# A windowed attention with block summaries and a four-expert attention layer: from a scheduled program to a recorded order of steps on fixed engines

## The chip, the cores and the metric

One core of a Trainium2 chip runs the whole program. The metric is the device time of one execution in microseconds. It is compared between two kernels that compute the same thing from the same inputs.

## The reference

Two layers follow each other. Batch 4, 8 heads, 768 positions, head size 64; the second layer has 4 experts of head size 64 over a model width of 512.

```
# layer 1, per head: local window plus block summaries
k_sum = k.reshape(B, H, 24, 32, D).max(axis=3)      # 24 blocks of 32 keys
v_sum = v.reshape(B, H, 24, 32, D).mean(axis=3)
scores = [where(|i - j| < 16, q k^T / 8, -1e9),  q k_sum^T / 8 + log(32)]
x = softmax(scores) @ [v, v_sum]                    # heads side by side: x is 768 x 512
# layer 2, per expert e: causal attention; a token uses its 2 best experts
logits = x @ w_gate;  w = softmax over the 2 largest logits
ye = softmax(causal(q_e k_e^T / 8)) @ v_e @ wo[e]   # q_e, k_e, v_e = x @ wq[e], wk[e], wv[e]
out = sum over the chosen e of w_e * ye
```

The choice of the two experts is exact in effect, so the kernels carry x as a half-precision high part and a low part (`xT_hi`, `xT_lo`), and the gate's logits use both.

## The kernel before

The kernel is written as Python loops over batches (L336). Each batch has a stage 1 (L114, layer 1) and a stage 2 (L215, layer 2). A scheduler places the instructions by data and by priority in program order; the engine of each instruction is the one that the code names, and the buffers come from pools with a fixed number per name (L52 to L56). PSUM has two tags of tiles: `one` (one bank, four buffers) and `two` (two banks, two buffers).

**Stage 1** works on head pairs, four per batch. For four heads at a time, v is loaded with 32 rows of a block per partition and reduced by a tree of five additions on GpSimd (L118 to L126): the block sums of v. Per pair, q and k are loaded and cast to half precision by GpSimd's DMA queue, one DMA per head (L133), in pieces of 256 bytes; windows of v (96 rows for each block of 64 queries) come by SP's queue (L142, L145), and the block sums are copied below them (L148). TensorE transposes q and k (L153, L158), VectorE copies them out of PSUM and takes the block maxima of k (`ksum`, L162). Scores are built in a two-bank tile per head: a mask is written by a matmul with the identity (L171), 12 local matmuls add the 96 keys of the windows (L178), and two matmuls with `ksum` as the stationary add the 24 summaries (L184). ScalarE takes the exponential of 120 rows (L188). The value matmul (L196) uses the exponentials as the stationary in fp32; VectorE normalises (L200, L201); TensorE transposes x (L206); ScalarE writes the high part (L209) and VectorE the low part (L210).

**Stage 2** projects values and gate logits (L224, L227), computes the gates in a chain of small VectorE steps with one exponential (L247 to L259), and handles two experts (`cc`) at a time: projections of q and k (L268), scores for three groups of key tiles and one expert after the other (L288), exponentials (L293), a causal select on the diagonal blocks by GpSimd (L298), the value matmuls (L307), normalisation times gate (L310 to L313), and transposes (L317). The output projection (L325) is copied by ScalarE or VectorE and stored by SP's queue (L332).

Stage 2's weights are loaded once, after stage 1 of batch 0 in program order, by GpSimd's queue with a cast (L83 to L99).

Of the kernel before, what the change touches and what calls it, by code (L numbers as in the profile page):

```python
# [8 lines left out]
FP32 = mybir.dt.float32  # L9
HALF = mybir.dt.float16  # L10
AL = mybir.AluOpType
# [19 lines left out]

GROUPS = [[(0, 0), (4, 768)], [(1, 0), (3, 640)], [(2, 0), (5, 512)]]
GBASE = [0, 1024, 2048]
GLEN = [1024, 1024, 640]
OFF2 = {tj: GBASE[g] + col for g, grp in enumerate(GROUPS) for tj, col in grp}

def win_start(t):
    return min(max(64 * t - 16, 0), S - WIN)
# [3 lines left out]
def kernel(  # L43
# [6 lines left out]
    nc = tc.nc  # L50

    consts = ctx.enter_context(tc.tile_pool(name="consts", bufs=1))  # L52
    xpool = ctx.enter_context(tc.tile_pool(name="xpool", bufs=2))
# [5 lines left out]
    ident16 = consts.tile((128, 128), HALF, name="ident16")  # L59
    make_identity(nc, ident16)  # L60
    ident32 = consts.tile((128, 128), FP32, name="ident32")
    make_identity(nc, ident32)

    maskb = consts.tile((128, NQ, 64), HALF, name="maskb")
    nc.gpsimd.memset(maskb, 0.0)
    for t0, t1 in ((0, 1), (1, NQ - 1), (NQ - 1, NQ)):
        shift = 64 * t0 - win_start(t0)
        m = maskb[0:WIN, t0:t1, :]
        n = t1 - t0

        nc.gpsimd.affine_select(m, m, [[0, n], [-1, 64]], AL.is_ge, NEG,
                                base=15 - shift, channel_multiplier=1)
        nc.gpsimd.affine_select(m, m, [[0, n], [1, 64]], AL.is_ge, NEG,
                                base=15 + shift, channel_multiplier=-1)

    wqk = consts.tile((128, NCH, 2, 2, 128), HALF, name="wqk")
    wvg = consts.tile((128, NCH, 264), HALF, name="wvg")
    wo_cat = [consts.tile((128, 512), HALF, name=f"wo_cat{cc}") for cc in range(2)]
    wg_f32 = consts.tile((128, NCH, 4), FP32, name="wg_f32")
    wg_hi32 = consts.tile((128, NCH, 4), FP32, name="wg_hi32")  # L80
    wg_lo32 = consts.tile((128, NCH, 4), FP32, name="wg_lo32")

    def load_stage2_weights():  # L83
        nc.sync.dma_start(out=wg_f32,
                          in_=moe_w_gate.rearrange("(c p) g -> p c g", p=128))
        for e in range(E):
            cc, ep = divmod(e, 2)
            for j, wsrc in enumerate((moe_wq, moe_wk)):
                nc.gpsimd.dma_start(out=wqk[:, :, cc, j, 64 * ep:64 * ep + 64],
                                    in_=wsrc[e].rearrange("(c p) d -> p c d", p=128))  # L90
            nc.gpsimd.dma_start(out=wvg[:, :, 64 * e:64 * e + 64],
                                in_=moe_wv[e].rearrange("(c p) d -> p c d", p=128))
        for cc in range(2):
            nc.gpsimd.dma_start(out=wo_cat[cc],
                                in_=moe_wo[2 * cc:2 * cc + 2].rearrange("e d n -> (e d) n"))
        nc.vector.tensor_copy(wvg[:, :, 256:260], wg_f32)
        nc.vector.tensor_copy(wg_hi32, wvg[:, :, 256:260])
        nc.vector.tensor_tensor(wg_lo32, wg_f32, wg_hi32, AL.subtract)
        nc.vector.tensor_scalar(wvg[:, :, 260:264], wg_lo32, LO_SCALE, None, AL.mult)  # L99
# [271 lines left out]
```

## Time and profile before

| | |
|---|---|
| runs, median (lowest to highest) | 301.04 us (299.4 to 301.61), 3 runs |
| profiled execution, span | 298.8 us |
| mean granted TensorE clock | 0.859 |
| TensorE / VectorE / ScalarE / GpSimd busy | 218.1 / 123.0 / 96.0 / 127.1 us |
| moved by DMA | 32.10 MB in 109,001 packets |

The span is the time from the first to the last instruction of the profiled execution; the page gives no other time for it. Busy time is the time in which an engine executes an instruction, and shares are of the span. The granted clock is a share of TensorE's full clock of 2.4 GHz: 1.00 is 2.4 GHz, 0.50 is 1.2 GHz, and numbers between them are a mean over the stretch. Matmuls are pipelined, so the start of one to the start of the next says more than the duration of one. "issue" is time in which an engine waited for nothing that the profile shows.

### The profile page before, as it was taken

Reading aid. Unit: us, or ns where it says so; the run is one execution under the profiler, and the core shown is the slowest. Engines: PE = TensorE matmul, PEld = TensorE weight load, DVE = VectorE, ACT = ScalarE, POOL = GpSimd, SP = SyncE. Lnnn points to the kernel's source line nnn. Section 1 sums busy time; section 2 is a strip of 40 time slices with the busy share of each in tenths; the row PEclk is TensorE's granted clock in tenths of the full one; section 3 lists DMA queues with packets and bytes.
Section 4 is the critical chain, followed back from the end, with each engine's and each line's share of the span. In section 5 each row is a group of like instructions: output and inputs, shape, how many; then the busy total and the mean of one; then the engine's idle time right before and its main releaser. Section 6 shows DMA issues by size and latency. Waiting matters only on the chain.

```text
span 298.8 us, 5906 instructions
## 1 busy us (share of the span) xinstructions
PE 218.1 (73%) x2448; PEld 140.8 (47%) x2448; DVE 123.0 (41%) x280; ACT 96.0 (32%) x117; POOL 127.1 (43%) x191
## 2 busy tenths in 40 slices
PE   1004998492678798877978888697789799679683
PEld 0002766360245466653544666462555566545340
DVE  0002655348042456654407366361425555461231
ACT  1001233205325433316261333307242433225612
POOL 7998543599603444892134249903024000003110
PEclk9999999867587999998675999976867999895957
DMA  7899999993920999939205999993009300000005
GB/s 199 124 81 173 169 168 191 135 119 50 176 49 0 155 232 220 171 79 177 56 0 39 309 225 103 157 184 70 2 0 133 133 2 2 2 0 2 0 0 211
DMA packets 109001, 32.10 MB, mean 107 GB/s; under 512 B 104880, under 2 KB 105136, under 8 KB 108208
## 3 DMA queue, kind: packets, MB, share of 16 engines
q0 software_dynamic: 56800, 7.35, 38.5%
q1 hardware_dynamic: 52176, 24.39, 37.7%
q8 instruction: 19, 0.31, 0.4%
q14 instruction: 6, 0.05, 0.1%
HBM read 30.42 MB, written 6.29 MB: 123 GB/s over the span
## 4 chain that ended last, share of the span: by engine, by line
PE 46%; DVE 22%; ACT 12%; POOL 9%; DMA 5%; issue 4%; SPq 0%; ACTq 0%; POOLq 0%
PE sp L288 7%; PE pp L268 6%; POOL v_s L123 6%; PE av L196 6%; PE av L307 6%; DVE xT_lo L210 5%; ACT a L293 4%; PE op L325 4%; PE sc L178 4%; ACT aT L188 4%; DVE ksum L162 4%; DVE x L201 4%; PE vp L224 3%; PE sc L171 3%; DMA v_s<-in_v_dram 3%
## 5 line engine op out<-in xcount | busy, mean ns | idle before, releaser
L298 POOL TENSOR_SCALAR_AFFINE_SELECT a<-a 128x256 f16<-128x256 f16 x48 | 19.4, 406 | 102.5 <-ACT a L293 102.5
L293 ACT ACTIVATE a<-sp 128x1024 f16<-128x1024 f32 (+1 forms) x48 | 41.2, 921 | 13.4 <-PE sp L288 13.4
L188 ACT ACTIVATE aT<-sc 120x768 f32<-120x768 f32 x32 | 25.5, 810 | 54.3 <-PE sc L184 54.3
L133 POOL DMA_DIRECT2D q_nat<-in_q_dram x32 | 26.9, 850 | 36.8 <-PE qT_ps L153 31.6
L123 POOL TENSOR_TENSOR v_s<-v_s 96x1024 f32<-96x1024 f32 (+4 forms) x40 | 40.6, 1023 | 3.4 <-DMA v_s<-in_v_dram 1.8
L288 PE MATMUL sp<-qkT,qkT 64*128 64x512 f16 (+3 forms) x128 | 27.8, 364 | 19.0 <-ACT a L293 10.4
L196 PE MATMUL av<-v_blk,aT 120*64 120x65 f32 x768 | 29.8, 231 | 5.1 <-ACT aT L188 2.9
L196 PEld LDWEIGHTS av<-v_blk,aT 120*64 120x64 f32 x768 | 25.9, 143 | 12.4 <-ACT aT L188 7.0
L307 PEld LDWEIGHTS <-a 128*128 128x128 f16 x336 | 20.3, 129 | 21.1 <-POOL a L298 17.8
L307 PE MATMUL av<-v,a 128*128 128x65 f16 x336 | 25.5, 242 | 5.1 <-POOL a L298 5.0
L209 ACT CAST xT_hi<-xT_ps 128x768 f16<-128x768 f32 x16 | 12.8, 798 | 47.4 <-PE xT_ps L206 47.4
L310 DVE RECIPROCAL r<-av 128x6 f32<-128x6 f32 x16 | 3.0, 190 | 60.6 <-PE av L307 60.6
L133 POOL DMA_DIRECT2D k_nat<-in_k_dram x32 | 26.7, 854 | 1.5 <-DMA k_nat<-in_k_dram 1.5
L200 DVE RECIPROCAL rec<-av 128x6 f32<-128x6 f32 x32 | 6.3, 196 | 50.5 <-PE av L196 50.5
L268 PE MATMUL pp<-xT_hi,wqk 128*128 128x512 f16 (+1 forms) x128 | 27.0, 358 | 0.0
L178 PEld LDWEIGHTS <-kT 64*96 64x96 f16 x384 | 18.8, 126 | 10.4 <-issue 5.7
L171 PE MATMUL sc<-maskb,ident 128*128 128x512 f16 x64 | 16.1, 337 | 10.3 <-DVE xT_lo L210 5.0
L178 PE MATMUL sc<-qT,kT 64*96 64x64 f16 x384 | 22.3, 212 | 0.6 <-DVE kT L160 0.6
L224 PE MATMUL vp<-wvg,xT_hi 128*128 128x264 f16 x96 | 19.1, 342 | 4.8 <-DMA wvg<-in_moe_wv_dram 3.1
L288 PEld LDWEIGHTS <-qkT 64*128 64x128 f16 x128 | 8.8, 98 | 28.0 <-issue 12.0
L153 PE MATMUL qT_ps<-ident,q_nat 128*128 128x128 f16 x96 | 9.4, 244 | 15.7 <-DMA q_nat<-in_q_dram 15.7
L325 PE MATMUL op<-wo_cat,wT 128*128 128x512 f16 x48 | 19.1, 536 | 1.1 <-DVE wT L319 0.7
(62 smaller groups left out, 272.1 us busy)
## 6 DMA issues: line engine op xcount, KB each, us to landing
v_blk<-in_v_dram SPq DMA_DIRECT2D x32, 240.0 KB
v_s<-in_v_dram SPq DMA_DIRECT2D x8, 768.0 KB
out_dram<-o_sb SPq DMA_DIRECT2D x12, 512.0 KB
q_nat<-in_q_dram POOLq DMA_DIRECT2D x32, 96.0 KB, 5.3
k_nat<-in_k_dram POOLq DMA_DIRECT2D x32, 96.0 KB, 6.5
v_blk<-v_s SPq DMA_DIRECT2D x32, 72.0 KB
v_blk<-in_v_dram SPq DMA_DIRECT2D x32, 48.0 KB
wqk<-in_moe_wq_dram POOLq DMA_DIRECT2D x4, 64.0 KB, 13.3
```

Of the source, the lines that this page charges most:

```text
L123: nc.gpsimd.tensor_tensor(v_s[:, 0:half], v_s[:, 0:half], v_s[:, half:2 * half], AL.add)
L133: nc.gpsimd.dma_start(out=dst[:, :, 64 * hp:64 * hp + 64], in_=src[b, 2 * c + hp].rearrange("(t p) d -> p t d", p=128))
L171: nc.tensor.matmul(sc[:, lo:hi], ident16, maskb.rearrange("p t n -> p (t n)")[:, lo:hi], start=True, stop=False, skip_group_check=True)
L178: nc.tensor.matmul(sps[hp][0:WIN, 64 * t:64 * t + 64], kT[rows, w0:w0 + WIN], qT[rows, 64 * t:64 * t + 64], start=False, stop=False, skip_ ...
L188: nc.scalar.activation(aT[0:KR, :], sps[hp][0:KR, 0:S], AF.Exp, scale=SCALE)
L196: nc.tensor.matmul(av[o:o + 64, t // 2, :], aTs[hp][0:KR, 64 * t:64 * t + 64], v_blk[0:KR, hp, t, :], start=True, stop=True)
L224: nc.tensor.matmul(vp[:, i, 0:264], xT_hi[ch][:, cols], wvg[:, ch, :], start=(ch == 0), stop=False, skip_group_check=True)
L268: nc.tensor.matmul(pp[:, lo:hi], wqk[:, ch, cc, j, :], xT_hi[ch][:, lo:hi], start=(ch == 0), stop=(ch == NCH - 1))
L288: nc.tensor.matmul(sp[:, c0:c0 + w], kT[rows, 128 * tj:128 * tj + 128], qT[rows, n0:n0 + w], start=True, stop=True)
L293: nc.scalar.activation(a2s[ep][:, base:base + ln], sp[:, 0:ln], AF.Exp, scale=SCALE / (XS * XS))
L307: nc.tensor.matmul(av2[:, ti, :], a2s[ep][:, o:o + 128], v2[:, tj, e, :], start=(tj == 0), stop=(tj == ti))
L325: nc.tensor.matmul(op[:, i, :], wavT[cc][:, 2 * t2 + i, :], wo_cat[cc], start=(cc == 0), stop=(cc == 1))
```

## The change

The loops and the scheduler's order are replaced by a list of 734 steps, each with the buffers that it reads and writes (`Plan`), and a table with one entry per step: its number, its engine (V VectorE, A ScalarE, G GpSimd, S SP, P TensorE) and the slots of the buffers that it opens. The steps are issued in the order of the table, and the scheduler is told to keep that order. The table interleaves stage 1 of a batch with stage 2 of the batch before. Copies that were always on one engine are divided among VectorE and ScalarE, and the additions of the v tree among GpSimd and VectorE.

The steps themselves change too. q and k are loaded four heads at a time, with 6 (q) or 8 (k) neighbouring positions in one partition, so that a piece is 1,536 or 2,048 bytes; a pair then needs 12 transposes for q and 16 for k, each filling 64 output partitions, and the copies out of PSUM put q's columns back in order. k stays in its order, and a copy (`kw`) gathers for each block of 64 queries its window of 96 keys, beside which the 24 block maxima are placed: one stationary of 128 columns. The summary matmuls go. The masks are matmuls over 64 rows per head. One DMA per pair loads the v windows of both heads. In stage 2 the score units are of at most 512 columns for both experts, whose matmuls alternate. Weights are loaded in fp32 by SP and cast by engines. PSUM is one tile of eight banks.

```diff
+UNITS = [[(0, 0, 512)], [(0, 512, 256), (4, 512, 256)], [(1, 128, 512)],
+         [(1, 640, 128), (3, 384, 384)], [(2, 256, 512)], [(5, 640, 128)]]
+UORDER = [0, 2, 4, 3, 1, 5]
...
+TABLE = """
+19,S,0 4,G, 5,V, 20,V, 17,G,0 88,P,0.0 6,G, 21,V, 8,G, 22,V, 68,P,1.1 0,G,1 18,G,0 89,V, 91,A,0 73,P,0.0 3,G,1
...
+    def emit(self, table):
...
+        for i, eng, slots in table:
...
+            st.fn(eng)
...
+                    nc.gpsimd.dma_start(
+                        out=T[name + "n"][t.slot][:, n * i:n * i + n, :],
+                        in_=src[b, h0:h0 + n].rearrange("h (p s) d -> p h (s d)", s=s))
...
+        def tk(e):
+            src = T["kn"][kn[b, g].slot]
+            for s in range(8):
+                for hp in range(2):
+                    nc.tensor.transpose(pbank16(kp)[64 * hp:64 * hp + 64, 96 * s:96 * s + 96],
+                                        src[:, hh + hp, 64 * s:64 * s + 64], T["id16"][0:96, 0:96])
...
+            copy(e, w[:, 1:NQ - 1, 0:WIN].rearrange("c t (p s) -> c t p s", s=8), src(6, 10, 8, 12))
...
+            copy(e, T["kw"][kw.slot][:, :, WIN:KR],
+                 T["ks"][ks.slot].unsqueeze(1).to_broadcast((128, NQ, NSUM)))
...
+                        nc.tensor.matmul(s[:, hp, 64 * t0:64 * t1], T["mt"][r, var, :],
+                                         T["pi"][r, t0:t1, :],
+                                         start=(i == 0), stop=False, skip_group_check=True)
+                for t in range(6):
+                    for hp in range(2):
...
+                        nc.tensor.matmul(s[:, hp, 64 * t:64 * t + 64],
+                                         T["kw"][kw.slot][r, tt, :],
+                                         T["qT"][qT.slot][r, 64 * tt:64 * tt + 64],
+                                         start=False, stop=True, skip_group_check=True)
...
+                    for tj, n0, w in UNITS[u]:
+                        for ep in range(2):
+                            r = slice(64 * ep, 64 * ep + 64)
+                            nc.tensor.matmul(pbank(sp, 2)[:, ep, c0:c0 + w],
+                                             T["qk"][qk[1].slot][r, 128 * tj:128 * tj + 128],
+                                             T["qk"][qk[0].slot][r, n0:n0 + w],
+                                             start=True, stop=True)
...
-    s1 = ctx.enter_context(tc.tile_pool(name="s1", bufs=2))
-    s2 = ctx.enter_context(tc.tile_pool(name="s2", bufs=2))
-    ps = ctx.enter_context(tc.tile_pool(name="ps", bufs=2, space=bass.MemoryType.PSUM))
...
+    ctx.enter_context(tc.manual_schedule())
...
+    T["ps"] = ps.tile((128, 8, 512), FP32, name="ps")
...
+    R = make_plan(nc, T, q, k, v, moe_w_gate, moe_wq, moe_wk, moe_wv, moe_wo, out)
+    R.emit(decode(TABLE))
```

## Rows read from the trace of the kernel before

**Rows 1.** The page: busy us of each engine, share of the span, instructions.

```profile
PE 218.1 (73%) x2448; PEld 140.8 (47%) x2448; DVE 123.0 (41%) x280; ACT 96.0 (32%) x117; POOL 127.1 (43%) x191
```

**Rows 2.** Stretches: length, busy us and instructions by engine, clock, DMA share, GB/s.

```profile
165.80:194.40 28.60, 23.49 (x376) 17.23 (x375) 15.01 (x29) 9.57 (x12) 19.92 (x22) 1.00 1.25 191
194.40:230.70 36.30, 30.70 (x238) 17.73 (x239) 14.40 (x41) 14.16 (x17) 8.28 (x17) 0.72 0.55 74
293.80:298.80 5.00, 0.00 (x0) 0.00 (x0) 0.00 (x0) 0.98 (x1) 0.00 (x0) 0.78 0.66 257
...
110.00:117.17 7.17, 6.42 (x100) 4.65 (x100) 4.29 (x8) 2.42 (x4) 3.29 (x4) 1.00 1.73 202
194.70:197.70 3.00, 3.00 (x25) 2.17 (x26) 0.83 (x3) 0.00 (x0) 0.00 (x0) 0.51 1.78 181
197.70:198.80 1.10, 1.10 (x21) 0.97 (x20) 0.84 (x3) 0.00 (x0) 0.00 (x0) 1.00 1.49 199
208.95:210.70 1.75, 1.75 (x33) 1.75 (x32) 0.56 (x3) 0.00 (x0) 0.28 (x1) 0.50 0.03 9
```

**Rows 3.** Timeline of the start: start, us, engine, line, operation, idle before.

```profile
6.61 2.33 POOL L123 TENSOR_TENSOR v_s<-v_s 96x1024 f32<-96x1024 f32 x1 [1.29 <-DMA v_s<-in_v_dram]
...
21.94 0.80 PE L153 MATMUL qT_ps<-ident,q_nat 128*128 128x128 f16 x6 [15.67 <-DMA q_nat<-in_q_dram]
```

**Rows 4.** Timeline of TensorE over one head pair.

```profile
109.93 0.72 PE L178 MATMUL sc<-qT,kT 64*96 64x64 f16 x12
110.58 0.49 PE L184 MATMUL sc<-qT,ksum 64*24 64x512 f16 x2
111.00 1.95 PE L196 MATMUL av<-v_blk,aT 120*64 120x65 f32 x48
112.88 0.51 PE L153 MATMUL qT_ps<-ident,q_nat 128*128 128x128 f16 x6
113.23 0.50 PE L158 MATMUL kT_ps<-ident,k_nat 128*128 128x128 f16 x6
113.96 0.84 PE L206 MATMUL xT_ps<-ident,x 128*128 128x128 f32 x6 [0.23 <-DVE x L201]
114.64 0.49 PE L171 MATMUL sc<-maskb,ident 128*128 128x512 f16 x2
```

**Rows 5.** The chain that ended last, two pieces: start, us, what.

```profile
209.15 1.76 PE av L307 x32
...
263.76 1.33 PE pp L268 x8
```

**Rows 6.** Groups by line, VectorE and ScalarE: busy us, mean ns, idle before.

```profile
L293 ACT ACTIVATE a<-sp 128x1024 f16<-128x1024 f32 x32 | 30.8, 1026 | 11.9 <-PE sp L288 11.9
L188 ACT ACTIVATE aT<-sc 120x768 f32<-120x768 f32 x32 | 25.5, 810 | 54.3 <-PE sc L184 54.3
L201 DVE TENSOR_TENSOR x<-av,rec 128x384 f32<-128x384 f32 x32 | 17.8, 557 | 1.1
L210 DVE TENSOR_TENSOR xT_lo<-xT_ps,xT_hi 128x768 f16<-128x768 f32 x16 | 15.3, 956 | 7.5 <-ACT xT_hi L209 7.4
L162 DVE TENSOR_REDUCE ksum<-kT 128x24 f16<-128x768 f16 x16 | 15.2, 953 | 0.5
L155 DVE COPY qT<-qT_ps 128x768 f16<-128x768 f16 x16 | 8.8, 550 | 22.9 <-PE qT_ps L153 22.8
```

**Rows 7.** Groups by line, GpSimd.

```profile
L298 POOL TENSOR_SCALAR_AFFINE_SELECT a<-a 128x256 f16<-128x256 f16 x48 | 19.4, 406 | 102.5 <-ACT a L293 102.5
L123 POOL TENSOR_TENSOR v_s<-v_s 96x1024 f32<-96x1024 f32 x8 | 18.9, 2362 | 1.8 <-DMA v_s<-in_v_dram 1.8
```

**Rows 8.** DMA: queues with packets, MB, share; issues with KB, us to landing.

```profile
q0 software_dynamic: 56800, 7.35, 38.5%
q1 hardware_dynamic: 52176, 24.39, 37.7%
...
k_nat<-in_k_dram POOLq DMA_DIRECT2D x32, 96.0 KB, 6.5
```

More of the change, by code (lines that the diff above doesn't have):

```diff
@@ L6 @@
 from concourse._compat import with_exitstack
-from concourse.masks import make_identity
 FP32 = mybir.dt.float32
@@ new lines, with __init__, buf, step @@
+class Plan:
+    def __init__(self):
+        self.steps = []
+    def buf(self, cls, n=1):
+        return Buf(cls, n)
+    def step(self, name, opts, reads, writes, fn, mode=0, dma=0.0, keep=()):
+        for x in set(reads) | set(writes) | set(keep):
+            x.left += 1
+        self.steps.append(Step(name, opts, reads, writes, keep, fn, mode, dma))
+    def emit(self, table):
+        held = set()
+        for i, eng, slots in table:
+            st = self.steps[i]
+            used = [x for x in dict.fromkeys(list(st.reads) + list(st.writes) + list(st.keep))
+                    if not x.cls.startswith(".")]
+            new = [x for x in used if x.slot is None]
+            assert len(slots) == len(new), st.name
+            for w, s in zip(new, slots):
+                w.slot = s
+                for k in range(w.n):
+                    assert (w.cls, s + k) not in held, (st.name, w.cls, s)
+                    held.add((w.cls, s + k))
+            st.fn(eng)
+            for x in set(st.reads) | set(st.writes) | set(st.keep):
+                x.left -= 1
+                if x.left == 0 and x.slot is not None:
+                    for k in range(x.n):
+                        held.remove((x.cls, x.slot + k))
@@ L42, with decode @@
+def decode(text):
+    out = []
+    for w in text.split():
+        i, e, s = w.split(",")
+        out.append((int(i), e, [int(x) for x in s.split(".") if x]))
+    return out
 @with_exitstack
@@ L336, with one, many @@
-    for b in range(B):
-        x = stage1(b)
-        if b == 0:
-            load_stage2_weights()
-        stage2(b, *x)
+    ctx.enter_context(tc.manual_schedule())
+    sb = ctx.enter_context(tc.tile_pool(name="sb", bufs=1))
+    ps = ctx.enter_context(tc.tile_pool(name="ps", bufs=1, space=bass.MemoryType.PSUM))
+    T = {}
+    def one(name, shape, dt):
+        T[name] = sb.tile(shape, dt, name=name)
+    def many(name, shape, dt):
+        T[name] = [sb.tile(shape, dt, name=f"{name}{i}") for i in range(SLOTS[name])]
@@ new lines @@
+    one("id16", (128, 128), HALF)
+    one("id32", (128, 128), FP32)
+    one("mt", (128, 3, 128), HALF)
+    one("pi", (128, 6, 64), HALF)
+    one("wqk", (128, NCH, 2, 2, 128), HALF)
+    one("wvg", (128, NCH, 264), HALF)
+    one("wo", (128, 2, 512), HALF)
+    one("wg32", (128, NCH, 4), FP32)
+    one("wgt", (128, NCH, 4), FP32)
+    many("qn", (128, 4, 384), HALF)
+    many("kn", (96, 4, 512), HALF)
+    many("kT", (128, S), HALF)
+    many("ks", (128, NSUM), HALF)
+    many("kw", (128, NQ, 128), HALF)
```

781 lines of the change are left out of this document (518 added, 263 removed).

## The prediction

> **What bounds the kernel now.** I read the page's engine shares first, because they say whether one engine is full. TensorE is busy 73% of the 298.8 us span, VectorE 41%, ScalarE 32%, GpSimd 43% [rows 1]. No engine is full, so the loss is in how the work is lined up, and the next view is the stretches [rows 2]. There each batch alternates: 28.6 us of stage 1 with TensorE 82% busy at granted clock 1.00, then 36 us of stage 2 with it 85% busy, but at clock 0.72. A busy TensorE at the lower of its two levels (1.2 instead of 2.4 GHz) is only half used, and the reader can see it on one kind of work: 25 matmuls of the value projections take 3.00 us at 0.51, and 21, mostly the same, 1.10 us at 1.00 [rows 2]. So stage 2 is long because ScalarE's exponentials and the copies make TensorE wait, and because the waiting lowers its clock. Last I read the start [rows 3]: both v loads are reduced on GpSimd ahead of its first q load, and the first transpose is at 21.94 us.
>
> **The change part by part.** I sum TensorE at clock 1.00, then add start, end and stalls; every instruction count is from the diff.
>
> *Stage 1, per head pair (16 pairs).* Now [rows 4]: 12 transposes at 0.35 us for six (112.88 to 113.23), 58 ns each; twice 0.42 masks, 0.65 for 12 local matmuls (109.93 to 110.58) and 0.42 summary (to 111.00; the masks have the same 768 columns), 2.98 together; 48 value passes in 1.95; output transposes 0.68. That is 6.3, beside 6.42 busy in 7.17 [rows 2].
> - Transposes become 28, each filling one half of the output partitions, 1,536 columns in each half. Below: the halves run side by side, 1,536 columns at 2.4 GHz, 0.64. Above: 28 x 58 ns, 1.62. The nearest row is the value matmul, which also alternates between output halves: 1.95 us / 48 = 40 ns, so I take 28 x 0.040 = 1.12. The Trainium skill's TensorEngine Tiling (Performance Considerations) says that column tiling switches off the fast weight load, and its page TensorE: Matmul & The Clock Gate (LDWEIGHTS) prices a load at columns/1.2 ns, an estimate of 53 ns here; by that this term would be 1.5 and the total some 6 us more, but the 40 ns of the value passes, 64 columns wide too, speak against it.
> - Scores: the four summary matmuls go (2 x 0.42), since a block's stationary now holds its 96 local keys and the 24 summaries. The 24 local ones stay, with 128 columns of weights instead of 96. Below, 64 columns at 2.4 GHz are 27 ns; above, 58; the row gives 54 (0.65/12). I take the middle, 40: 0.97. Masks: the same 1,536 columns, but each over half the rows: 0.32 (side by side) to 0.84 (today); I take 0.42. Together 1.4, bounds 0.96 and 2.2.
> - Values 1.95 and output transposes 0.70 stay.
>
> Sum 1.12 + 1.4 + 1.95 + 0.70 = 5.17, bounds 4.25 and 6.5; 16 pairs: 83 us (68 to 104), today about 101.
>
> *Stage 2, per batch.* Value projections: two tiles fill 1.10 us at 1.00 [rows 2], so six take 3.3. Projections 4 x 1.33 = 5.3; output 12 x 512 columns at their rate (3,072 columns in 1.33 us), 2.7 [rows 5]. Expert values: 32 matmuls take 1.76 us at clock 0.50 [rows 2, 5], so 28 ns each at 1.00, and 84 x 0.028 = 2.3. Transposes 0.7. Scores: 2 x 5,376 columns; one after the other at the projections' rate 4.6, with the two experts' halves (now issued alternately) side by side 2.3; no row of before shows which, and I take the middle, 3.4. Sum 17.7, bounds 16.6 and 18.9; four batches 71 us (66 to 76).
>
> TensorE: 154 us, bounds 134 and 180.
>
> *What lies beside it.* VectorE: 16 normalisations and 8 weighted outputs at 2 x 0.557, 16 low parts at 0.956, 16 maxima at 0.953, 17 f16 copies at 0.550, 16 f32 ones at 0.956, five output copies of 1,024 columns (1.27 at that rate) are 90; 17 tree adds, five gathers, seven value casts and the gates bring some 38 more: 128 us. ScalarE: 40 exponentials at 1.026, 8 short ones, 32 at 0.810, 39 copies at the same rate, seven output copies, four gathers: 120 [rows 6]. GpSimd: 48 selects at 0.406, seven gathers, 23 tree adds (2.36 for the widest) and 18 load issues instead of 64: about 86 [rows 7], against 127.1 now. Each is below TensorE's 154, so they cost nothing as sums; they cost as waits.
>
> New and unseen is the gather that builds the stationary, 1,120 f16 elements with strided reads. The maximum's row (768 strided f16 elements in 0.953) makes it 1.4 on VectorE. On GpSimd the rows lie at a select of 256 f16 in 0.406 (1.8) and an f32 add of 1,024 in 2.36 (2.6) [rows 7]; I take 2.4, nearer the add. It stands between kT and the scores of every pair. By these prices kT's copy and the gather take 1.9 to 3.2 us, and the recorded order puts 2.9 to 22.6 us of other TensorE work between a pair's k transposes and its first score in 15 of 16 pairs (1.6 in the third pair, the first to reach its values), so it is covered; without that cover each pair would pay some 2 us, 32 in all. What queues behind a gather on GpSimd are tree adds, load issues and diagonal selects, for which expert value matmuls wait: at most one gather, 2.4 us, late.
>
> *Loads and queues.* Most of the software queue's 56,800 packets [rows 8] go: rows of 1,536 and 2,048 bytes replace 256-byte ones. The v windows keep their 256-byte packets, so the other queue stays near 37.7% of 299 us, 113 us of DMA time, in a shorter span: about 60%, not a bound. SP also takes over 13 weight loads from GpSimd, and their casts follow as four copies on VectorE and GpSimd; stage 1 of batch 0 hides both, and if it did not, the first projections would wait for a landing, 6.5 us for a load of like size [rows 8]. A store in SP's queue waits for its output copy with the next pairs' v loads behind it and their value matmuls behind those: a late copy, 1.3 us, passes on in full only where the four v buffers have run dry.
>
> *Start.* The first k load now stands behind one identity, at about 1.2 us; with 6.5 us to landing [rows 8] transposes begin near 8. v's tree is split over VectorE and GpSimd; its load lands at 6.61 [rows 3], five adds and one more transfer follow, and values start near 13. I charge 8 us of nothing and 4 of half speed: 12. *End.* From the last output matmul to the end is 5.0 us today [rows 2], and stays. The last batch's stage 2 has no stage 1 beside it: its last normalisation, transposes and copies expose some 4 us.
>
> *Stalls.* In today's stage 1, 0.75 of 7.17 us is TensorE waiting [rows 2]. Three engines at 154, 128 and 120 in fixed queues will hardly do better: 10% of 154, 15. (Cutting the recorded order into 12 or 24 equal stretches and taking the fullest engine of each gives 3 to 12 us over TensorE's own sum.)
>
> Sum: 154 + 12 + 5 + 4 + 15 = 190 us of span. The runs shown are 299.4 to 301.6, median 301.0, against this execution's span of 298.8, so 2 us lie around it: **192 us**.
>
> **Rivals.**
> - *Halves side by side.* If TensorE runs row and column halves at once, its sum is the lower bound: 134 + 36 + 2 = 172. For it: the 40 ns of a value pass are less than today's 58. Against: no row shows two halves overlapping, and VectorE's 128 then bounds nearly as soon. The Trainium skill's TensorEngine Tiling (Key Properties) says that different tiles can load and multiply in parallel, which is this rival's mechanism. 0.25.
> - *Half clock again.* If the fixed queues leave TensorE waiting as today's stage 2 does, the mixed order loses its clock too: stage 2's busy time was 30.7 at 0.72 [rows 2] against about 19 at full clock, so up to 4 x 10 to 12 us more: 230. For it: today's clock is at 0.50 wherever exponentials have paced TensorE [rows 2]. Against: the order now sets stage 1 steps between the score units. 0.20.
> - *One PSUM tile, one chain* (slower). All eight banks are now one tile. If waits are kept for the tile and not for its banks, every group of matmuls waits for the last reader of any bank. Then TensorE's 154 and the PSUM readers (ScalarE: 112 of its 120) alternate, with some 0.2 us of handover for each of 232 groups, 46; with start, end and the 2 us, 331. It decides as soon as groups in different banks can't be open at once. Against: every step addresses banks of its own, and no two open groups share one. 0.03.
>
> **How the numbers follow.** Forecast 0.50, side by side 0.25, half clock 0.20, one chain 0.03, and 0.02 for losses that just eat the gain. A change within 1% can't be told from none here. So faster 0.95, within 1% 0.02, slower 0.03. Range: from below the side-by-side case, 168, to near half clock, 225, which also holds the upper TensorE bound (180 + 38 = 218); outside lie the chain and the worst of half clock.
>
> **What would show it.** First transpose near 8 us; clock 0.9 or more between 20 us and the last batch; a pair's transposes 1.1 and a score half 0.7 us; two score matmuls of 512 columns starting together (side by side) or 0.2 us apart; TensorE busy near 155 us, 80%. Wrong would be stretches of clock 0.5 in the middle, matmuls that wait for readers of other banks, or VectorE above 90%.

## The result, and the profile after

The changed kernel takes **208.11 us** (median of 4 runs, 206.85 to 211.19) against 300.22 us (297.81 to 301.61) of the kernel before in the same session: a ratio of 0.692, 95% interval 0.687 to 0.698. The forecast was 192 us in a range of 168 to 225. The profiled execution took 208.41 us with a span of 206.4 us, so again 2 us lie around the span. Ratios, here and below, leave out runs in the chip's slower state (here the 211.19), so they can differ a little from the quotient of the medians. Four of the forecast's terms were off, in both directions, and the experiments are about those.

The page's engine shares, as [rows 1] before (busy us, share of the span, instructions). PE are TensorE's matmuls and PEld its weight loads; DVE is VectorE, ACT ScalarE, POOL GpSimd and SP SyncE:

```profile
PE 149.7 (73%) x2704; PEld 115.2 (56%) x2704; DVE 131.6 (64%) x227; ACT 123.1 (60%) x152; POOL 82.8 (40%) x146
```

VectorE was forecast at 128, ScalarE at 120, GpSimd at 86 and TensorE at 154 us. All four are within 4% of that, and still the span is 16 us longer than the 190 forecast. TensorE's share, 73%, is the very share it had before: it waits for the same share of a shorter time. Where it waits is in the stretches (as [rows 2]: length, busy us and instructions of PE, PEld, DVE, ACT and POOL, granted clock, DMA share, GB/s):

```profile
0.00:24.00 24.00, 6.88 (x136) 5.53 (x136) 9.03 (x15) 13.95 (x12) 12.82 (x44) 1.00 1.03 175
24.00:40.00 16.00, 10.50 (x180) 9.32 (x182) 10.31 (x9) 3.29 (x5) 7.00 (x9) 1.00 1.02 146
40.00:100.00 60.00, 43.62 (x866) 35.76 (x861) 36.27 (x70) 34.76 (x44) 20.79 (x27) 0.94 1.16 191
100.00:160.00 60.00, 49.84 (x983) 38.11 (x981) 48.21 (x76) 39.08 (x52) 33.55 (x44) 0.97 0.91 167
160.00:195.00 35.00, 34.84 (x529) 24.58 (x526) 24.24 (x55) 29.02 (x37) 8.64 (x23) 1.00 0.29 72
195.00:206.40 11.40, 4.02 (x26) 1.92 (x24) 3.56 (x7) 3.04 (x3) 0.00 (x0) 0.87 0.62 230
```

Read the last two columns beside the first. From 160 us, with the DMA engines 29% busy, TensorE is idle for 0.2 of 35 us. In all the time before, the DMA share is 0.91 to 1.16, and TensorE is idle for 22.6 of the first 40 us and for 26.5 of the next 120. The last 11.4 us hold another 7.4. (A share near 1 is not a limit reached: packets of both queues count, and it is 2.03 at the start of the version with narrow loads, experiment 8.) Set against the forecast's terms:

| us of span | forecast | measured |
|---|---|---|
| TensorE busy | 154 | 149.7 |
| start (idle before 40 us) | 12 | 22.6 |
| stalls (idle 40 to 195 us) | 15 | 26.7 |
| end (idle after 195 us) | 9 | 7.4 |
| sum | 190 | 206.4 |

The two queues, as [rows 8] (packets, MB, time of the packets as a share of 16 engines' span). q1 is SP's, with the v windows (tile `vb`), v for the block sums (`vs`), weights and stores; q0 is GpSimd's, with k and q (`kn`, `qn`):

```profile
q1 hardware_dynamic: 58016, 26.48, 67.4%
q0 software_dynamic: 7456, 6.29, 20.2%
```

q0 lost 49,344 packets, as the diff says. q1 gained 5,840, nearly all of them the weights'. Its 67.4% of 206.4 us are 139 us of packet time. Of these 122 us fall before 160 us (the same line for that part of the span):

```profile
q1 hardware_dynamic: 52320, 21.40, 76.4%
```

That is not even either: q1's share is 29% in the first 24 us, where q0 has 74%, then 91% until 100 us and 77% from there to 160. Nor does q1 always have work. From 91.9 to 105.45 us SP issues nothing, because the block-sum copies that are next in its order wait for the tree on GpSimd, and q1's share from 98 to 105 us is 2% (SP's waits: us, times, longest):

```profile
SPq L286 <- POOL vs L247: 18.8, 3, 10.9
```

Most packets, 52,192 of 58,016, are 256-byte rows of windows, block sums and weights, at a mean of 28 ns of an engine each; the 768 rows of 8,192 bytes for the block sums take 534 ns each.

TensorE's timeline shows what became of the scores (start, recorded us, line, operation; L361 are masks, L368 local scores with summaries, L582 expert scores):

```profile
67.70 0.39 PE L582 MATMUL ps<-qk,qk 64*128 64x256 f16 x4
67.93 0.33 PE L361 MATMUL ps<-pi,mt 64*128 64x320 f16 x4
68.09 0.34 PE L368 MATMUL ps<-qT,kw 64*128 64x64 f16 x12
68.27 0.33 PE L361 MATMUL ps<-pi,mt 64*128 64x64 f16 x4
68.43 0.34 PE L368 MATMUL ps<-qT,kw 64*128 64x64 f16 x12
```

Read the starts, since the recorded durations overlap: from 67.93 to 68.27 one half needs 0.34 us, half of the 0.7 forecast. Twelve matmuls of 64 columns start in 0.18 us, 15 ns each, where 64 columns at 2.4 GHz need 27: two run at a time. The trace agrees with the rule in the Trainium skill's TensorEngine Tiling (Array Packing), Key Properties, that tiles work in parallel. Taking the two row halves in turns is not all of it: the kernel before did so too, at 54 ns for each of its twelve [rows 4]. Experiment 8 shows a part of the rest.

The transposes and values, in three other places:

```profile
109.59 0.53 PE L334 MATMUL ps<-id,qn 128*64 128x128 f16 x12
109.95 0.51 PE L296 MATMUL ps<-id,kn 96*64 96x96 f16 x16
110.40 0.45 PE L582 MATMUL ps<-qk,qk 64*128 64x128 f16 x4
...
140.00 1.57 PE L385 MATMUL ps<-vb,aT 120*64 120x65 f32 x48
```

A pair's transposes take 0.81 us (109.59 to 110.40) instead of 1.12, its 48 value passes 1.57 at most instead of 1.95. With output transposes at the 0.70 forecast and two score halves a pair costs 3.8 us (0.81 + 0.68 + 1.57 + 0.70), below the 4.25 of the lower bound. The Trainium skill's TensorEngine Tiling (Array Packing), Restrictions, says that column tiling disables the fast weight load; at the price of a load that its page TensorE: Matmul & The Clock Gate (LDWEIGHTS) gives, 28 loads one after the other were to take an estimated 1.5 us. The measured 0.81 decides against that sum, but not against the price: 14 loads in each half, with both halves at work at once, would be an estimated 0.74.

The start of the timeline, as [rows 3] (start, us, engine, line, operation, idle before and what ended it):

```profile
8.24 1.49 PE L296 MATMUL ps<-id,kn 96*64 96x96 f16 x32 [8.24 <-DMA kn<-in_k_dram]
...
11.25 1.83 SPq L286 DMA_DIRECT2D vb<-vs  x2
...
13.12 0.54 SPq L268 DMA_DIRECT2D vb<-in_v_dram  x1
13.71 7.28 SPq L240 DMA_DIRECT2D vs<-in_v_dram  x1
...
27.28 1.57 PE L385 MATMUL ps<-vb,aT 120*64 120x65 f32 x24 [5.57 <-DMA vb<-in_v_dram]
```

The first transpose is at 8.24 us, as forecast ("near 8"), but the first value matmul only at 27.28, not "near 13". Its v window was asked for at 13.12, since SP issues in order and the block-sum copy ahead of it waited for the tree until 11.25, and the window needed 14.03 us to land, beside q0's loads of k and q. The issue right behind it held SP for 7.28 us. Later waits for loads come back, in the waits (engine and line, what they waited for: us, times, longest) and in the chain that ended last (start, us, what):

```profile
POOL vs L247 <- DMA vs<-in_v_dram: 20.7, 2, 15.9
...
PE ps L385 <- DMA vb<-in_v_dram: 7.1, 2, 5.6
...
PE ps L385 <- DMA vb<-vs: 6.9, 3, 4.2
```

```profile
13.12 14.03 DMA vb<-in_v_dram
...
77.25 13.53 DMA vb<-vs
```

Last, the copies, as [rows 6] (group, busy us and mean ns):

```profile
L161 ACT COPY qT<-ps 128x768 f16<-128x768 f16 x10 | 15.6, 1612 | 0.1
...
L163 POOL COPY kw<-kT 128x960 f16<-128x960 f16 x7 | 12.9, 1839 | 11.6 <-PE ps L368 8.1 <-ACT kT L161 3.5
L163 DVE COPY qT<-ps 128x768 f16<-128x768 f16 x6 | 12.9, 2145 | 12.4 <-PE ps L334 12.2
```

The gather on GpSimd, bounded from afar, came out as taken: 1.84 and a second piece of 0.47, against 2.4. The q copies did not. I priced 16 of them at 0.81 and 0.956 and missed that in even batches they write every sixth element: those take 2.7 to 2.9 us, those of odd batches 0.80 (ScalarE) and 0.94 (VectorE).

### The profile page after: what moved, and what is told of

Same layout as the page of the kernel before. It is cut to its first block, busy times and chain, and to the rows that moved or that the text cites. A ratio compares the mean times of both kernels' runs of the same rounds, so it can differ in the third digit from the quotient of the medians.

```text
span 206.4 us, 6279 instructions
## 1 busy us (share of the span) xinstructions
PE 149.7 (73%) x2704; PEld 115.2 (56%) x2704; DVE 131.6 (64%) x227; ACT 123.1 (60%) x152; POOL 82.8 (40%) x146
## 3 DMA queue, kind: packets, MB, share of 16 engines
q1 hardware_dynamic: 58016, 26.48, 67.4%
## 4 chain that ended last, share of the span: by engine, by line
PE 41%; DVE 21%; DMA 17%; issue 10%; ACT 6%; SPq 1%; POOL 1%; DVEq 0%; POOLq 0%; ACTq 0%
PE ps L385 9%; PE ps L558 7%; DMA vb<-in_v_dram 7%; DMA vb<-vs 7%; DVE qT L163 4%; PE ps L410 4%; PE ps L493 4%; PE ps L647 4%; PE ps L582 3%; DMA kn<-in_k_dram 3%; DVE ks L305 3%; PE ps L334 2%; PE ps L606 2%; PE ps L296 2%; DVE x L400 2%
## 5 line engine op out<-in xcount | busy, mean ns | idle before, releaser
L590 ACT ACTIVATE a<-ps 128x1024 f16<-128x1024 f32 (+1 forms) x48 | 42.0, 915 | 14.1 <-PE ps L582 12.6
L385 PE MATMUL ps<-vb,aT 120*64 120x65 f32 x768 | 30.1, 241 | 14.7 <-DMA vb<-in_v_dram 7.1
L247 POOL TENSOR_TENSOR vs<-vs 96x1024 f32<-96x1024 f32 (+4 forms) x23 | 25.3, 1100 | 31.4 <-DMA vs<-in_v_dram 20.7
L385 PEld LDWEIGHTS ps<-vb,aT 120*64 120x64 f32 x768 | 27.8, 154 | 17.5 <-issue 11.9
L375 ACT ACTIVATE aT<-ps 120x768 f32<-120x768 f32 x32 | 25.2, 819 | 14.2 <-PE ps L368 11.3
L558 PE MATMUL ps<-hi,wqk 128*128 128x384 f16 x128 | 22.6, 326 | 1.6 <-ACT aT L375 1.6
L163 POOL COPY kw<-kT 128x960 f16<-128x960 f16 (+1 forms) x14 | 15.7, 1153 | 11.6 <-PE ps L368 8.1
L410 PE MATMUL ps<-id,x 128*128 128x128 f32 x96 | 16.8, 320 | 4.5 <-issue 1.6
L421 DVE TENSOR_TENSOR lo<-ps,hi 128x768 f16<-128x768 f32 x16 | 15.4, 971 | 5.2 <-ACT hi L161 5.0
L361 PE MATMUL ps<-pi,mt 64*128 64x64 f16 (+1 forms) x128 | 12.8, 271 | 7.0 <-issue 3.3
L410 PEld LDWEIGHTS ps<-id,x 128*128 128x128 f32 x96 | 12.7, 162 | 6.6 <-issue 2.1
L247 DVE TENSOR_TENSOR vs<-vs 96x512 f32<-96x512 f32 (+4 forms) x17 | 10.5, 615 | 8.9 <-DMA vs<-in_v_dram 7.0
L582 PE MATMUL ps<-qk,qk 64*128 64x512 f16 (+3 forms) x128 | 14.6, 307 | 2.1 <-DVE x L400 1.2
L368 PE MATMUL ps<-qT,kw 64*128 64x64 f16 x384 | 12.8, 204 | 4.2 <-ACT qT L161 2.3
L161 ACT COPY qT<-ps 128x768 f16<-128x768 f16 x10 | 15.6, 1612 | 0.1
```

The lines of the kernel that those rows point to most:

```text
L161: nc.scalar.copy(dst, src)
L163: en(e).tensor_copy(dst, src)
L247: en(e).tensor_tensor(w[:, 0:half], w[:, 0:half], w[:, half:2 * half], AL.add)
L375: nc.scalar.activation(T["aT"][aT.slot][0:KR], pbank(sc, 2)[0:KR, :, 0:384], AF.Exp, scale=SCALE)
L385: nc.tensor.matmul(pbank(av, 2)[o:o + 64, u, 65 * (2 * (t // 2) + hp):65 * (2 * (t // 2) + hp) + 65], a[0:KR, hp, 64 * t:64 * t + 64], T[" ...
L410: nc.tensor.transpose(pbank(xp, 2)[:, t // 3, 128 * (t % 3):128 * (t % 3) + 128], T["x32"][x32.slot][:, 128 * t:128 * t + 128], T["id32"])
```

## The experiments

Theory **A**: q1 moves its packets as fast as it can until about 140 us, and TensorE waits for what is late on it. Rivals: **B**, the copies and reductions of VectorE and ScalarE set the pace; **C**, a third cause, which differs between the expectations: engines waiting for each other in the fixed order (1, 2), an order that asks for loads later than it could (6, 7), or TensorE's own time (8). Ratios are against the kernel before, run in the same session.

**1. The q copies in one form.** Even batches too write in a row and read every sixth element; it is the same permutation, walked in the other order.

```
-            if b % 2:
-                copy(e, dst.rearrange("c (p s) -> c p s", s=6),
-                     src.rearrange("c (s p) -> c p s", s=6))
-            else:
-                copy(e, dst.rearrange("c (p s) -> c s p", s=6),
-                     src.rearrange("c (s p) -> c s p", s=6))
+            copy(e, dst.rearrange("c (p s) -> c p s", s=6),
+                 src.rearrange("c (s p) -> c p s", s=6))
```

> The copy that puts q's columns back in order is written in two forms: in odd batches it writes neighbouring elements and reads with a stride (0.80 us on ScalarE, 0.94 on VectorE), in even batches it reads neighbouring ones and writes every sixth (2.73 to 2.92). Here all 16 use the first form. Theory A (SP's one queue of 256-byte pieces sets the time until about 140 us): at most 4 us less, 204 to 207. Theory B (the slow q copies on VectorE and ScalarE set it): eight copies at 1.9 us come off the path, 15 us less, 193. Theory C (engines wait for each other in the fixed order, whatever the loads and copies cost): nothing that can be told, 206 to 209.

203.7 us (203.06 to 204.57), ratio 0.679 [0.674, 0.684]: 4 us, 0.3 us past A's range and far from B's 193. The copies, in the form of the group list above:

```profile
L161 ACT COPY qT<-ps 128x768 f16<-128x768 f16 x10 | 7.8, 799 | 0.5 <-PE ps L334 0.5
...
L163 DVE COPY qT<-ps 128x768 f16<-128x768 f16 x6 | 5.7, 953 | 14.8 <-PE ps L334 14.7
```

Of 28.5 us of q copies 15.0 fall away on the two engines, and some 4 us of time: the copies are mostly, not wholly, beside other work. The start gains nothing: scores are ready sooner, and the first values wait longer for the same window, until 29.58 us. Of the versions that leave nothing out this is the fastest.

**2. The v windows loaded only once per buffer.** 4 of 16 window loads stay.

```
         def dv(e):
+            if vb.slot in loaded:
+                return
+            loaded.add(vb.slot)
```

> The v windows are loaded only the first time that each of the four buffers is used: 4 loads of 2,304 pieces instead of 16, so later pairs use the windows of earlier ones. Theory A: 27,600 of the queue's 58,016 pieces go, the waits for window and block-sum transfers (14 us of TensorE in all, and the work that they delay) go with them, 180 to 190 us. Theory B: 203 to 207. Theory C: 203 to 207.

197.99 us (194.93 to 199.04), ratio 0.653 [0.645, 0.662]. q1 falls by 27,840 packets:

```profile
q1 hardware_dynamic: 30176, 19.40, 43.3%
```

10 us by the medians and 12 by the ratios, between A's 180 to 190 and the rivals' 203 to 207. The windows are a cause, but not the only thing that is late: the longest entry left in the middle of the chain was 11.29 us of a q load. And the start is not touched, since its windows are first loads; the first values are at 28.04.

**3. No load twice.** As 2, with q, k and the v of the block sums too; the weights, block-sum copies and stores stay.

```
                 def go(e, t=t, src=src, name=name, s=s, i=i):
+                    if (name, t.slot, i) in loaded or parts == 1 and (name, t.slot, 1) in loaded:
+                        return
+                    loaded.add((name, t.slot, i))
...
+            if ("vs", t.slot) in loaded:
+                return
+            loaded.add(("vs", t.slot))
```

> All loads of q, k, v windows and v for the block sums are made only the first time a buffer is used (5 of 16 windows' loads and so on stay; later pairs compute with the data of earlier ones), the weights, block-sum copies and output stores stay. It is the floor that the recorded order has without repeated loads. Theory A (loads are what holds the middle of the kernel): the idle 26 us of TensorE between 40 and 160 us fall to under 10, 180 to 190 us. Theory B (the copies and reductions of the vector and scalar engines hold it): as without the windows alone, 196 to 199 us. In both the start stays: the first value matmuls after 24 us, 20 us idle on TensorE before 40 us.

188.55 us (188.02 to 189.18), ratio 0.633 [0.629, 0.638]. A's range held. The stretches:

```profile
0.00:24.00 24.00, 6.88 (x136) 5.51 (x136) 9.02 (x15) 13.92 (x12) 12.14 (x43) 1.00 0.98 165
24.00:40.00 16.00, 9.66 (x196) 8.79 (x198) 10.76 (x10) 3.68 (x6) 6.22 (x8) 0.89 0.87 142
40.00:100.00 60.00, 51.46 (x1007) 39.87 (x1006) 48.13 (x88) 47.22 (x61) 26.73 (x33) 1.00 0.26 63
100.00:160.00 60.00, 54.77 (x1121) 42.42 (x1119) 51.79 (x85) 41.96 (x55) 27.63 (x41) 1.00 0.26 71
160.00:180.00 20.00, 18.67 (x253) 12.21 (x250) 12.57 (x31) 15.03 (x19) 4.78 (x12) 1.00 0.22 80
```

From 40 to 160 us the DMA share is 0.26, the clock 1.00, and TensorE is idle 13.8 us instead of 26.5 (not "under 10"). Its busy time over the whole run is 141.9 us instead of 149.7, so the 19.8 us of span are 12.7 of these waits and 7.8 of busy time, less 0.9 that the start was worse. The 0.94 and 0.97 of clock that the changed kernel was granted in those stretches, after the waits, are thus part of what the loads cost. From 40 to 180 us TensorE is idle for 15.1 us, about the stalls that the forecast allowed: what it left out is the loads. This run takes away the packets and every wait for them together, so it can't say whether the queue's rate or the moment at which the order asks for a load made them late.

**4. The first window ahead of the block sums.** Only the order on SP's queue is changed at the start.

```
 recorded order:  dvs01 ... ds02 ... dv02 ... dvs00 ... ds03, dv03
 tried:           dvs01, dv02 ... ds02, dv03 ... dvs00 ... ds03
```

> In SP's order the first pair's v windows (pair 0,2) stand behind the block sums' copy, which waits for v's tree until 11.25 us; TensorE's first value matmul waits for those windows until 27.3 us. Here that load goes ahead of the copy, right behind the first v load; nothing else changes (the next pair's windows follow the copy directly). Theory S (the start is long because of this place in the queue): the first values come near 18 us and the time falls by 7 to 10 us, 198 to 201. Theory A (the queue's rate sets it, whatever the order): the load takes as long beside the k and q loads, 205 to 208.

208.07 us (206.38 to 208.32), ratio 0.698 [0.691, 0.704]: no difference. The start of TensorE:

```profile
11.18 1.49 PE L289 MATMUL ps<-id,kn 96*64 96x96 f16 x32 [11.18 <-DMA kn<-in_k_dram]
...
24.50 1.57 PE L378 MATMUL ps<-vb,aT 120*64 120x65 f32 x24
```

The values come 2.8 us earlier, and the k transposes 2.9 us later, since k's packets now share the engines with the window's; then the second v load lands at 32.2 us. What one load gains the next one pays, as A says, but across the two queues: k's load is on q0 and the window's on q1.

**5. Part of the windows on GpSimd's queue.** The odd pairs' windows of batches 1 to 3.

```
-            nc.sync.dma_start(out=w[0:WIN, t0:t1, 0:64], in_=src)
+            q_ = nc.gpsimd if c % 2 and b else nc.sync
+            q_.dma_start(out=w[0:WIN, t0:t1, 0:64], in_=src)
```

> The v windows of every second pair of batches 1 to 3 go to GpSimd's queue instead of SP's; six loads, 13,800 pieces of 256 bytes. Theory A (one queue is too full between 40 and 140 us): 200 to 204 us. Rival: GpSimd, which now waits for a free v buffer in its fixed order, holds up diagonal selects and k, q loads behind that: 208 to 216.

230.38 us (229.69 to 231.28), ratio 0.774 [0.768, 0.781]: 22 us slower, outside of both ranges. q1 loses 13,824 packets and falls to 49.9% of the span, and q0 gains only 960, because on it most of the same bytes travel in packets of 4,096. But GpSimd computes as well, in order (its line beside TensorE's):

```profile
113.20 2.35 POOL L247 TENSOR_TENSOR vs<-vs 96x1024 f32<-96x1024 f32 x1
...
115.50 1.21 POOL L269 DMA_DIRECT2D vb<-in_v_dram  x1
...
124.00 1.62 PE L386 MATMUL ps<-vb,aT 120*64 120x65 f32 x48 [0.60 <-DMA vb<-in_v_dram]
```

The window is asked for after the tree add that stands ahead of it, and its values start 8.5 us after that. From 100 to 195 us TensorE is idle for 24.9 us (95 - 44.5 - 25.6), where it was for 10.3. So what q1 gains was lost again in GpSimd's order; how the 22 us divide over its adds, selects and loads was not taken apart, and whether a relieved q1 alone would help is not shown.

**6. Everything from batch 1 on asked for as soon as its buffer is free.** In the recorded order the last pair's buffer is zeroed at the start and kept for it, so three of the four `vb` buffers rotate. Here four do, and each window moves up to where its buffer comes free.

```
 recorded: zv33 at step 107; dv11 178, dv10 219, dv12 232, dv13 251, ... dv22 475, dv32 594
 tried:    zv33 just before dv33; dv11, dv10, dv12, dv13 at 175 to 178, dv21 189, ... dv22 269, dv32 484
```

> The order of the steps as in the changed kernel, but the last pair's buffer of v windows is no longer zeroed at the start, so that four buffers rotate instead of three, and from batch 1 on each window is asked for as soon as its buffer is free, its block sums as soon as they are summed. Theory C (the loads are late because the recorded order issues them a few steps before their use): the 10 us that fell away without the repeated windows come back as time saved, 196 to 201 us. Theory A (until about 140 us the queue of the synchronous engine moves its packets as fast as it can, so an earlier request only makes another load late): 205 to 209 us, with the block-sum loads or the q and k loads late in the windows' place. Theory B (what waits is set by the vector and scalar engines): 206 to 209 us.

234.99 us (233.3 to 235.9), ratio 0.789 [0.782, 0.796]: 27 us slower, outside of every theory's range. The queue and the waits show what the earlier windows displaced:

```profile
55.67 10.80 SPq L261 DMA_DIRECT2D vb<-in_v_dram  x4
...
79.36 0.47 SPq L441 DMA_DIRECT2D a<-in_moe_wv_dram  x1
```

```profile
POOL vs L240 <- DMA vs<-in_v_dram: 53.7, 4, 19.1
...
POOL wvg L156 <- DMA a<-in_moe_wv_dram: 18.8, 1, 18.8
```

The last weight of the value projections, at 61.38 us in the changed kernel, is asked for at 79.36, behind five windows, and GpSimd waits 18.8 us for it; the loads of the block sums cost GpSimd 53.7 us of waiting instead of 20.7. The direction is A's (what is asked for early makes something else late), but the size is also that of my placing: I moved windows past the weights without asking which of the two was due first. Whether a better placed early order would gain was not tried.

**7. The same, with the block sums' loads early too and the q copies of experiment 1.**

> As the kernel before in this list (four buffers, windows as early as their buffers allow), and the loads for the block sums too are asked for as soon as their buffer is free; and all copies of transposed q write in a row and read every sixth element, which alone was worth 4 us. Theory C: both gains add, 190 to 197 us. Theory A: only the copies' 4 us are left, 201 to 205 us. Theory B: with cheaper copies, 200 to 204 us.

220.93 us (220.22 to 221.47), ratio 0.742 [0.735, 0.749]: outside of all three ranges. It is better than 6 by 14 us, with q copies that alone gave 4, and GpSimd's waits for the sum loads fall from 53.7 to 21.9 us, so the early sum loads do help there; but C's 190 to 197 is refuted for this placing as well. GpSimd still waits 22.2 us in one piece before the value weights' cast.

**8. The parts of the change.** Narrow loads: q and k are loaded in 256-byte rows as before, in their natural order, with copies that read and write in a row.

```
-                        in_=src[b, h0:h0 + n].rearrange("h (p s) d -> p h (s d)", s=s))
+                        in_=src[b, h0:h0 + n].rearrange("h (s p) d -> p h s d", s=s))
...
+            copy(e, dst, src)
```

> q and k are loaded in pieces of 256 bytes again (one position per partition and row, four heads at a time), so their columns come out of the transposes in order: the q copy, the k maxima and the gather read neighbouring elements. The software queue gets 43,000 pieces more. If the wide pieces carry a part of the gain (the loads then take longer and come late): 214 to 225 us. Rival: the loads are hidden and the re-ordering is what costs (8 q copies of 2.73 us, the gather): 196 to 204 us.

210.99 us (210.13 to 213.84), ratio 0.708 [0.700, 0.716], some 3 us more, between the two ranges. The software queue goes back to 49,440 packets and 57.8%, and the two queues together have a DMA share of 2.03 in the first 24 us; VectorE and ScalarE are 22 us less busy between them (120.2 and 112.2). So the wide loads are worth some 3 us net; they save packets and cost strided copies, and with the copies of experiment 1 the distance is 7 us.

Separate summaries: a block's stationary holds its local keys alone, and the summaries get a matmul of 384 columns per head and half.

```
-                        nc.tensor.matmul(s[:, hp, 64 * t:64 * t + 64], T["kw"][kw.slot][r, tt, :], ...
+                        nc.tensor.matmul(s[0:WIN, hp, 64 * t:64 * t + 64], T["kw"][kw.slot][r, tt, 0:WIN], ...
+                for hp in range(2):
+                    nc.tensor.matmul(s[WIN:KR, hp, 0:384], T["kw"][kw.slot][r, 0, WIN:KR], ...
```

> One part of the change undone: a block's stationary holds only its 96 local keys, and the 24 summaries get one matmul of 384 columns per head and half, as the kernel before had it; order, buffers and loads as in the changed kernel. It adds two matmuls of 384 columns to each of the 32 score halves. Eight such matmuls take 1.31 us in the changed kernel's projections, 0.164 us each, so a half grows by 0.16 us where its two heads run side by side and by 0.33 us where they do not: 5 to 10.5 us of TensorE. Theory C (TensorE's own time sets the end): 213 to 219 us. Theory A (before 160 us TensorE waits for loads, and what it does there is covered): 207 to 211 us, with TensorE's busy time up and its idle time down by about the same.

211.01 us (208.62 to 216.02), ratio 0.701 [0.696, 0.706], against 0.692 [0.687, 0.698]: some 1%, with intervals that overlap. The page:

```profile
PE 164.1 (79%) x2768; PEld 122.2 (59%) x2768; DVE 132.6 (64%) x227; ACT 124.0 (60%) x152; POOL 84.3 (41%) x146
```

TensorE is busy for 14.4 us more and idle for 13.0 us less (207.8 - 164.1 = 43.7 against 56.7). Most of the work added to TensorE vanishes in its waits, as A's expectation has it, so until 160 us TensorE's own time is not what holds the kernel; after that, idle for 0.2 of 35 us, it is. The 14.4 us are more than the 5 to 10.5 expected. A half takes 0.81 us here (117.48 to 118.29) instead of 0.34:

```profile
117.48 0.34 PE L361 MATMUL ps<-pi,mt 64*128 64x320 f16 x4
117.66 0.43 PE L368 MATMUL ps<-qT,kw 64*96 64x64 f16 x12
118.02 0.33 PE L374 MATMUL ps<-qT,kw 64*24 64x384 f16 x2
118.29 0.39 PE L587 MATMUL ps<-qk,qk 64*128 64x256 f16 x4
```

The summaries are 0.27 of it. The rest is that the twelve local matmuls, with a stationary of 96 columns, need 0.36 us until the next group starts; with 128 columns they needed 0.18. How much of that is the width and how much the change to another kind of matmul behind it is not separated. The wider stationary, whose price the forecast set between 27 and 58 ns a matmul, thus comes with the lowest one, 15.

The recorded order: all the new steps in the order of the program, on the recorded engines, once with the scheduler free to move them and once fixed.

```
-    ctx.enter_context(tc.manual_schedule())        (the first of the two only)
...
-        for i, eng, slots in table:
+        for i in range(len(self.steps)):           (buffers: the free one that was longest unused)
```

> As the run in program order (439 us), but the scheduler may move instructions by data and priority as it did for the kernel before; engines and slots stay as in program order. If the new steps carry a part of the gain by themselves: 230 to 270 us. If the slots in program order forbid the overlap, or the gain is the recorded order's alone: 300 us or more.

> The same 734 steps on the same engines, issued in the order in which the program lists them (a batch's stage 1, then its stage 2), each buffer taking the slot that has been free longest. If the recorded order carries the gain: as today's stages follow each other, 255 to 285 us. If the new steps carry it: 210 to 225. Theory A: near 235, since the queue has stage 2's time to run ahead.

Moved by the scheduler 307.91 us (307.19 to 309.06), ratio 1.035 [1.024, 1.045]; fixed 438.99 us (434.85 to 440.12), ratio 1.459 [1.444, 1.474], outside of every range that was expected of it. The page of the scheduler's version:

```profile
PE 195.5 (64%) x2704; PEld 140.6 (46%) x2704; DVE 131.6 (43%) x227; ACT 123.2 (40%) x152; POOL 84.1 (27%) x146
```

The same 2,704 matmuls keep TensorE busy 195.5 us at a mean clock of 0.81, and 223.7 us at 0.71 in the fixed order, against 149.7 at 0.97. In these two orders, then, the new steps are worth nothing; the recorded table is worth the whole 100 us, and 45.8 of them are longer busy time of the same matmuls, at a lower clock. The table holds the slots too, and both runs give them out in program order: how much of the 100 us is the order of the steps and how much the slots is not separated.

**9. One half after the other.** Masks, local scores and expert scores are issued for all blocks of one head, then of the other.

```
...
-                for t in range(6):
-                    for hp in range(2):
+                for hp in range(2):
+                    for t in range(6):
...
```

> The matmuls of the two heads (scores of stage 1) and of the two experts (scores of stage 2) are issued one half after the other instead of alternately; nothing else changes. If the alternating halves run side by side, TensorE's sum grows by about 9 us in stage 2 (5,376 columns per expert pair at 2.4 GHz, twice as long) and some 5 to 10 in stage 1. As predicted (TensorE is the bound): 220 to 227 us. Theory A: most of it is hidden in waits for the queue until 140 us and shows only after that, 209 to 214. If the halves never ran side by side: no change, 208.

208.07 us (205.2 to 208.95), ratio 0.688 [0.679, 0.697]: no difference. By the expectation that was to mean that the halves never ran side by side; the starts show that they do, in this order of issue too:

```profile
119.08 0.35 PE L368 MATMUL ps<-qT,kw 64*128 64x64 f16 x10
119.26 0.27 PE L582 MATMUL ps<-qk,qk 64*128 64x256 f16 x1
119.27 0.22 PE L368 MATMUL ps<-qT,kw 64*128 64x64 f16 x2
```

In the single records one half's matmuls start 29 ns apart (119.08, 119.11, 119.14), and from 119.15 the other half's start between them. The row at 119.26 is an expert score, which stands behind all twelve in the program; it starts before the last two of the second half. So each half goes through its own matmuls and does not wait for the other, and the order within a group needs no care here.

## Why the prediction was right, and where it was wrong

- **Faster, by about a third: right,** and for the step named first: stage 1 steps set between the score units keep the clock. It was 0.94 to 1.00 from 40 to 195 us, where stage 2 had 0.72 [rows 2]; the half-clock rival (230 us) did not come, and with the table's order and slots taken out (experiment 8) the clock fell to 0.81 and 0.71. The forecast's reading that today's clock is at 0.50 wherever exponentials have paced TensorE was too narrow: the 0.51 at 194.70 us comes before the first exponential of that batch's expert scores (203.16), and behind 4.7 us in which TensorE was busy for 2.45.
- **One PSUM tile, one chain (331 us): not seen.** Mask and score matmuls of one pair run between the expert scores of another batch (67.70 to 68.43 above), in other banks and with no wait, while ScalarE reads PSUM in three exponentials (66.09 to 69.15).
- **"Halves side by side" (0.25): its mechanism is what happens,** its 172 us are not. Transposes, masks and scores run two at a time, and the dense price of a pair is 3.8 us against the 5.17 taken. The forecast held that no row showed two halves overlapping and kept to a middle price; that step was wrong. In busy time it made little: 149.7 us, forecast 154. A group that stands alone still shows its full 0.33 us where 0.16 would do in a row, and the clock was below 1.00 at times. So the agreement is partly luck: the pair's price was 1.4 us too high, some 22 us over 16 pairs, and what stood against it was not foreseen and not taken apart.
- **"About 60%, not a bound": the step that failed.** The forecast set q1's 113 us against the whole span and charged nothing for its loads. Measured are 139 us, 122 of them before 160 us, and a share of 91% from 24 to 100. The repeated loads cost 12.7 us of waits (the stalls were 11.7 over the forecast) and 7.8 of busy time (experiment 3). That loads are the cause is shown by that run; that q1 moves its packets as fast as it can is not, since it stands nearly empty from 98 to 105 us while SP waits for the tree. How much is the queue's rate and how much the order in which SP asks stays open.
- **"Values start near 13": wrong by 14 us,** the start's 12 being 22.6. I took the k load's 6.5 us to landing [rows 8] and counted the tree; I didn't add up what is in flight. By 24 us some 4.2 MB had been moved (24 us at 175 GB/s), at a share of 1.03, most of it q0's k and q loads (2.7 MB). The first window took 14.03 us to land beside them, and putting it first moved the delay to k (experiment 4). What the start could be with fewer bytes was not tried.
- **q copies at 0.81 and 0.956: wrong for the even half,** 2.7 to 2.9 us; 4 us in the end (experiment 1).
- **GpSimd, the gather, the end: right** (82.8 for 86; 2.31 for 2.4; 7.4 for 9). The stalls of 15, meant for engines in fixed queues, compare with the 15.1 that are left when the repeated loads are out of the way; what those consist of was not taken apart. (The items that the forecast lists for VectorE's 90 add up to 88.)
- **"Wrong would be ... VectorE above 90%":** it is at 64%, and the experiment that took 4 us of its work and 8 of ScalarE's gave 4.

What stays open: whether an order that keeps each load's due time, with four window buffers, would win back some of the 12 us; experiments 6 and 7 only show two that don't.

## What to carry to other kernels

Set a queue's packet time against the stretch in which its loads are wanted, not against the span: 67% on average was 91% from 24 to 100 us and 37% after 160. On a busy queue asking earlier need not help, because a load that moves up can push another back, as in experiments 4, 6 and 7; so look at which is due first and at how many packets can be saved. And when work is added to an engine and the time hardly moves, that engine isn't the bound there, however busy its row on the page looks.

## What the runs showed of the hardware

- Writing every sixth f16 element was dear, reading it much less: 768 elements a partition from PSUM took 2.7 to 2.9 us on either engine when written 12 bytes apart; read 12 bytes apart and written in a row they took 0.80 on ScalarE and 0.95 on VectorE (experiment 1); in a row on both sides 0.80 and 0.55 to 0.56 (narrow loads).
- One DMA issue held SP for 7.28 us, at 13.71 right behind a window of 2,304 rows, though its record names no semaphore that it waits for; the window's own issue took 0.54.
- 256-byte packets on q1 took 28 ns of an engine each, as a mean, and 22 with most loads gone (experiment 3). On GpSimd's queue six windows of such rows went in 960 packets instead of 13,824 (experiment 5).
- Matmuls that fill half of the rows each ran two at a time, at 15 ns for 64 columns when issued in turns. Issued one half after the other, each half still started one in 29 ns, and a half could be in the next group before the other had finished (experiment 9).
- Twelve local matmuls with a stationary of 128 columns needed 0.18 us, with one of 96 columns 0.36 until the next group (experiment 8).
